# 906 more elements rest in free PSUM columns, and two loads are cut finer, in a decode kernel whose DMA engines never stop

## The chip, the cores and the metric

The kernel runs on one core of one Trainium2 chip. The metric is the device time of one execution in microseconds; lower is better. Times scatter by a few tenths of a microsecond between runs. Words used: HBM is the large memory that the loads read; SBUF and PSUM are the core's own memories; PSUM, divided into banks, takes the results of matmuls. In the views PE is TensorE (PEld its weight loads), DVE VectorE, ACT ScalarE, POOL GpSimd, SPq the queue of SyncE, which issues the loads. A load has landed when its last packet is in.

## The reference

Two layers, each attention and then a gated MLP, for one token. Only the last 4,096 positions of the caches count. Both layers use the same weights and the same caches.

```python
def _A_ref(x, k_cache, v_cache, wq, wo):            # Hq = Hkv = 32, Dh = 192, W = 4096, D = 640
    q = (x @ wq).reshape(B, Sq, Hq, Dh).transpose(0, 2, 1, 3)
    k = k_cache[:, :, Sk - W:, :]; v = v_cache[:, :, Sk - W:, :]
    p = softmax(einsum("bhqd,bhkd->bhqk", q, k) * Dh ** -0.5)
    return einsum("bhqk,bhkd->bhqd", p, v).transpose(...).reshape(B, Sq, Hq * Dh) @ wo
def _B_ref(x, w_gate, w_up, w_down):                # F = 1536
    return (sigmoid(x @ w_gate) * (x @ w_up)) @ w_down
x = A_x
for _ in range(2):
    x = x + _A_ref(layernorm(x), ...)
    x = x + _B_ref(layernorm(x), ...)
```

## The kernel before

Heads are treated in 16 pairs. A pair needs its query weights and keys ("a") and its values and output weights ("b"); each is about 7 MB for all 128 partitions. The bytes go by one DMA queue, issued by SyncE, into seven slots of SBUF and one region for the MLP's weights, cut into cells of 640 columns (`FW`). Some pairs stay in SBUF for layer 1. Of pair 1's values a part stays as well: it is copied into PSUM columns that nothing else uses ("stow"), and copied back in layer 1.

```python
stash = [(bank[i][:, c:c + n].bitcast(U32), 2 * n) for i, c, n in ((3, 0, NST // 2), (6, 0, NST // 2), (7, DC, 512 - DC))]
NSV = sum(n for _, n in stash)                      # 480 + 480 + 507 words: 2,934 bf16 elements a partition
...
MW = {..., "u2": (6, 7, 10), "u3": (9, 10, 12), "d2": (11, 6, 9), "d3": (14, 9, 12)}   # first cell, from block, to block
MV = {"v1": (17, len(rc)), "v0": (NSV // FW, 6), "v2": (6, 11), "v3": (11, 14), "v4": (14, 17)}   # cells of pair 1's values
VAFTER = {"v1": "u1", "v0": "d1", "v2": "u3", "v3": "d2", "v4": "d3"}     # issued when this piece of the MLP is consumed
...
def stow(i, after=()):                              # VectorE copies a part of pair 1's values out
    sv, o = B_SLOT[0][PM], sum(n for _, n in stash[:i])
    ev = pg.op("dve", lambda v: words(v, stash[i][0], slot(sv, v_at(PM) + o, stash[i][1])), rd=[rval[sv]], wr=[res(f"stash{i}")], own="st", after=after)
    rslot[sv].rd.append(ev)                         # the next load into this slot waits for the copy
def step(p, prev):
    if l == 0 and prev > 0:
        ev = PVn(prev - 1, 1 - prev % 2)            # output projection; frees the slot
    Q(p, 0); QK(p, 0); soft(0)
    if (l, prev) == (0, PM):                        # PM = 1
        stow(2, [ev])
    expo(); PVmm(prev, prev % 2); ET(p % 2); PVt(prev % 2)
    ...
def loop(p0, n):
    ...
            step(p + 1, p)
            if (l, p) == (0, PM):
                stow(0)
                stow(1)
```

A load into a slot is issued when all that used the slot is done. It then stands in the queue behind the bytes that were issued before it.

## Time and profile before

The kernel took 514.38 us (median of 3 runs). First the page of the kernel before: span, engine shares, the DMA row of the 40 slices (tenths busy), the packets, the bytes from HBM and the chain of waits by engine.

```profile
span 512.7 us, 8581 instructions
PE 263.9 (51%) x3716; PEld 138.7 (27%) x3716; DVE 100.3 (20%) x379; ACT 85.0 (17%) x171; POOL 4.2 (1%) x31
DMA  9999999999999999999999999999999999999996
DMA packets 9964, 218.71 MB, mean 427 GB/s; under 512 B 1240, under 2 KB 1368, under 8 KB 4952
HBM read 218.43 MB, written 0.00 MB: 426 GB/s over the span
DMA 63%; PE 24%; DVE 7%; ACT 3%; SPq 2%; issue 2%; DVEq 0%; POOL 0%; ACTq 0%; POOLq 0%
```

No compute engine is busy much over half of the time, and the DMA row is nines to the last slice. The DMA engines are the bound. The trace has a record of each packet with its start, its duration and its size. From these records, by packet size (bytes of one row), the median duration; the last column is what 16 engines move at that rate:

```
bytes of a packet   median us   x16 GB/s
            1,812       0.075        387
            2,560       0.102        402
            3,840       0.149        412
            6,400       0.244        420
           56,832       2.098        433
```

This is 8.4 ns plus 0.0368 ns a byte, to within 2 ns. A load of 128 rows puts 8 such packets and a semaphore write of 9 ns on each of the 16 engines. Between 5 and 506 us the engines have 16 packets in flight at every moment, to within 0.05 us.

Next the chain of waits of the kernel before, near the copies out and at the end (start, duration, what), and from the queue's own waits the one on a copy (total, times, longest).

```profile
55.67 0.22 DVE sh L511
55.90 1.14 DVE bank L170 x2
57.05 22.51 DMA big<-in_uc_dram
...
485.35 24.70 DMA big<-in_wd_dram
510.10 0.46 PE o L748 x6
```

```profile
SPq L214 <- DVE bank L170: 0.5, 1, 0.5
```

The two copies of line 170 end at 57.03 us, and only then is the next load issued. It lands 22.5 us later, behind the bytes that were issued before. The last load lands at 510.05 us; what follows is short and fixed.

### The profile page before, as it was taken

The page shows a single profiled execution, that of the slowest core. Times are in us where ns is not written, and L with a number is a line of the kernel's source. Part 1 is how long each engine was busy: PE and PEld are TensorE (multiplying, and loading weights), DVE is VectorE, ACT ScalarE, POOL GpSimd, SP SyncE. Part 2 cuts the span into 40 slices and gives each one's busy share as a digit, 9 for nine tenths or more (in the row PEclk, how much of TensorE's full clock was granted, in tenths as well). Part 3 has the DMA queues.
Part 4 walks back from the last instruction along what each step waited for, and adds up shares of the span by engine and source line. Part 5 has one row for each costly group of instructions (what it writes and reads, how often), then busy time and mean ns, then how long its engine had stood idle before and what let it go on. Part 6 is the DMA issues. An engine that isn't in the chain of part 4 may idle for free.

```text
span 512.7 us, 8581 instructions
## 1 busy us (share of the span) xinstructions
PE 263.9 (51%) x3716; PEld 138.7 (27%) x3716; DVE 100.3 (20%) x379; ACT 85.0 (17%) x171; POOL 4.2 (1%) x31
## 2 busy tenths in 40 slices
PE   0362455344643254445565777774625344634665
PEld 0221222122312122222234434532312122312334
DVE  0221212112210121112121243321202111210311
ACT  1110111011110111011120024130301011101220
POOL 0010000000000000000000000000000000000000
PEclk9955665566565775556575568765755566556565
DMA  9999999999999999999999999999999999999996
GB/s 431 426 423 426 427 430 428 430 461 439 426 430 426 435 430 426 443 457 430 394 420 415 419 438 441 434 425 425 461 439 435 426 426 430 445 426 417 427 429 273
DMA packets 9964, 218.71 MB, mean 427 GB/s; under 512 B 1240, under 2 KB 1368, under 8 KB 4952
## 3 DMA queue, kind: packets, MB, share of 16 engines
q1 hardware_dynamic: 9800, 218.37, 99.1%
q8 instruction: 13, 0.21, 0.1%
q10 hardware_dynamic: 144, 0.06, 0.0%
q14 instruction: 7, 0.06, 0.0%
HBM read 218.43 MB, written 0.00 MB: 426 GB/s over the span
## 4 chain that ended last, share of the span: by engine, by line
DMA 63%; PE 24%; DVE 7%; ACT 3%; SPq 2%; issue 2%; DVEq 0%; POOL 0%; ACTq 0%; POOLq 0%
DMA big<-in_uc_dram 54%; PE scores L430 8%; PE o L487 7%; DMA big<-in_wd_dram 6%; DMA big<-in_wu_dram 3%; DVE sc L440 3%; PE bank L446 2%; SPq L214 2%; PE bank L412 2%; ACT e_sb L454 2%; PE bank L522 1%; PE bank L460 1%; ACT diag L443 1%; DVE sc L472 1%; DVE qs L418 1%
## 5 line engine op out<-in xcount | busy, mean ns | idle before, releaser
L430 PE MATMUL scores<-big,qs 128*32 128x512 bf16 x744 | 82.9, 613 | 10.3 <-DVE qs L418 9.6
L412 PE MATMUL bank<-sh,big 128*128 128x1 bf16 x465 | 17.1, 166 | 132.5 <-DMA big<-in_uc_dram 130.1
L487 PE MATMUL o<-big,et_sb 128*2 128x384 bf16 x1024 | 78.1, 471 | 5.4 <-DMA big<-in_uc_dram 4.2
L443 ACT ACTIVATE diag<-cst,sc 128x128 f32<-128x128 bf16 x32 | 12.8, 401 | 307.9 <-DVE sc L440 292.3
L440 DVE TENSOR_REDUCE sc<-scores 128x1 f32<-128x1024 f32 x31 | 37.9, 1224 | 78.9 <-PE scores L430 78.9
L412 PEld LDWEIGHTS bank<-sh,big 128*128 128x128 bf16 x465 | 14.7, 104 | 135.6 <-DMA big<-in_uc_dram 113.4
L446 PE MATMUL bank<-diag,sc 128*128 128x128 f32 x64 | 22.7, 452 | 47.2 <-ACT diag L443 47.2
L454 ACT ACTIVATE e_sb<-scores,sc 128x1024 bf16<-128x1024 f32 x31 | 37.3, 1204 | 42.1 <-DVE sc L449 39.7
L487 PEld LDWEIGHTS o<-big,et_sb 128*2 128x2 bf16 x1024 | 28.6, 108 | 42.1 <-issue 29.8
L418 DVE TENSOR_TENSOR qs<-bank,cst 128x96 bf16<-128x96 f32 x30 | 7.7, 258 | 162.5 <-PE bank L412 162.5
L430 PEld LDWEIGHTS scores<-big,qs 128*32 128x32 bf16 x744 | 24.4, 133 | 43.8 <-issue 31.4
L446 PEld LDWEIGHTS bank<-diag,sc 128*128 128x128 f32 x64 | 14.2, 277 | 72.3 <-ACT diag L443 71.1
L494 ACT CAST o_sb<-o 128x384 bf16<-128x384 f32 x64 | 29.8, 473 | 21.2 <-PE o L487 21.0
L522 PE MATMUL bank<-sh,big 128*128 128x1 bf16 x480 | 17.1, 165 | 15.1 <-DVE sh L511 14.7
L464 DVE CAST et_sb<-bank 128x64 bf16<-128x64 f32 x32 | 7.2, 225 | 70.2 <-PE bank L460 70.2
L522 PEld LDWEIGHTS bank<-sh,big 128*128 128x128 bf16 x480 | 14.5, 99 | 17.6 <-DVE sh L511 12.3
L447 DVE TENSOR_REDUCE sc<-bank 128x2 f32<-128x128 f32 x32 | 9.3, 292 | 41.9 <-PE bank L446 41.9
L460 PEld LDWEIGHTS bank<-cst,e_sb 128*128 128x128 bf16 x256 | 8.9, 101 | 22.8 <-issue 16.3
L460 PE MATMUL bank<-cst,e_sb 128*128 128x8 bf16 x256 | 11.7, 169 | 6.6 <-ACT e_sb L454 6.5
L470 PE MATMUL o<-sc 128*128 128x2 f32 x62 | 13.8, 292 | 0.6 <-ACT o_sb L494 0.6
L470 PEld LDWEIGHTS o<-sc 128*128 128x128 f32 x62 | 11.9, 240 | 1.9 <-ACT o_sb L494 1.3
L472 DVE RECIPROCAL sc<-o 64x1 f32<-64x1 f32 x62 | 10.2, 164 | 9.4 <-PE o L470 7.7
(78 smaller groups left out, 107.8 us busy)
## 6 DMA issues: line engine op xcount, KB each, us to landing
big<-in_uc_dram SPq DMA_DIRECT2D x20, 7104.0 KB, 22.6
big<-in_uc_dram SPq DMA_DIRECT2D x11, 3552.0 KB, 21.4
big<-in_uc_dram SPq DMA_DIRECT2D x2, 3072.0 KB, 18.0
big<-in_uc_dram SPq DMA_DIRECT2D x7, 480.0 KB, 6.6
big<-in_uc_dram SPq DMA_DIRECT2D x4, 768.0 KB, 11.6
big<-in_uc_dram SPq DMA_DIRECT2D x1, 2048.0 KB, 11.1
big<-in_uc_dram SPq DMA_DIRECT2D x1, 2016.0 KB, 10.4
big<-in_wg_dram SPq DMA_DIRECT2D x4, 480.0 KB, 14.6
```

The source lines that it names most:

```text
L412: ins = t.matmul(qe[:, i:i + 1], lhsT=w[:, c * 2 * DH + c0:c * 2 * DH + c0 + P], rhs=xq[:, c:c + 1], start=(c == 0), stop=(c == DC - 1))
L430: ins = t.matmul(sc_x[1 + b][32 * j:32 * j + 32, :], lhsT=qs[:, y, k, :], rhs=slot(sa, WQE + k * W + (4 * b + j) * 512, 512), start=(k == ...
L440: pg.op("dve", lambda v: v.reduce_max(out=mx, in_=sc_x[0][:], axis=AX.X), wr=[res("mx")], ex=sc_x[3:5])
L443: pg.op("act", lambda a: a.mul(out=diag[:], in_=ident, mul=mx), rd=[res("cst"), res("mx")], wr=[res("diag")])
L446: pg.op("pe", lambda t: t.matmul(dmx[:, 0:P], lhsT=ones_f, rhs=diag[:], start=True, stop=True), rd=[res("diag"), res("ones")], ex=[rb[2]])
L454: pg.op("act", lambda a: a.activation(out=e_sb[:], in_=sc_x[0][:], func=ACT.Exp, bias=nbias, scale=srs_c, accum_out=rowsum), rd=[res("nbia ...
L460: ins = t.matmul(qe[:, 0:2 * NB].rearrange("p (r x) -> p r x", r=2)[:, :, 4 * b:4 * b + 4], lhsT=e_sb[:, b * P:(b + 1) * P], rhs=sel, star ...
L470: pg.op("pe", lambda t: t.matmul(sm, lhsT=ones_f, rhs=rs2[z], start=True, stop=True), rd=[res(f"rs2{z}"), res("ones")], wr=[res("rsum")], ...
L472: rb[bk].last["dve"] = pg.op("dve", lambda v, h=h: v.reciprocal(out=Rn[z][64 * h:64 * h + 64], in_=sm[64 * h:64 * h + 64, h:h + 1]), rd=[r ...
L487: ins = t.matmul(o8[h][32 * j:32 * j + 2, 0:2 * DH].rearrange("p (a d) -> p a d", a=2), lhsT=et_sb[:, z, h * NB + 2 * u:h * NB + 2 * u + 2 ...
L494: pg.op("act", lambda a, h=h: a.copy(out=o8_sb[:, :, h * DH:(h + 1) * DH], in_=o8[h][:, 0:2 * DH].rearrange("p (a d) -> p a d", a=2)), wr= ...
L522: ins = t.matmul(yT[:, j:j + 1], lhsT=wo[:, c * D + j * P:c * D + (j + 1) * P], rhs=oTb[z][:, c:c + 1], start=False, stop=(c == 2), skip_g ...
```

## The change

Its intent is fewer bytes. Three further ranges of PSUM columns (453 words) in banks 2, 4 and 5, which attention uses, take 906 elements of pair 1's values, so that the load "v0" of those elements falls away. The values that follow, and the last piece of the down weights, are loaded in smaller pieces, so that the queue is fed at shorter intervals. The new ranges must be copied back earlier in layer 1, before their banks are used.

```diff
-    stash = [(bank[i][:, c:c + n].bitcast(U32), 2 * n) for i, c, n in ((3, 0, NST // 2), (6, 0, NST // 2), (7, DC, 512 - DC))]
+    SB = [(3, 0, NST // 2), (6, 0, NST // 2), (7, DC, 512 - DC), (2, 264, 248), (4, 2 * DH + 2, 126), (5, 2 * DH, 79)]
+    stash = [(bank[i][:, c:c + n].bitcast(U32), 2 * n) for i, c, n in SB]
@@ loads
-          ... "d3": (14, 9, 12)}
+          ... "d3": (14, 9, 11), "d4": (16, 11, 12)}
-    MV = {"v1": (17, len(rc)), "v0": (NSV // FW, 6), "v2": (6, 11), "v3": (11, 14), "v4": (14, 17)}
-    VAFTER = {"v1": "u1", "v0": "d1", "v2": "u3", "v3": "d2", "v4": "d3"}
+    MV = {"v1": (17, len(rc)), "v0": (6, 9), "v2": (9, 11), "v3": (11, 14), "v4": (14, 17)}
+    VAFTER = {"v1": "u1", "v0": "u2", "v2": "u3", "v3": "d2", "v4": "d4"}
@@ copies out, layer 0 (soft calls `late` between its last two VectorE steps)
-            soft(0)
+            soft(0, late=(lambda: stow(3)) if (l, prev) == (0, PM) else None)
             if (l, prev) == (0, PM):
                 stow(2, [ev])
@@
                     if (l, p) == (0, PM):
-                        stow(0)
-                        stow(1)
+                        for i in (0, 1, 4, 5):
+                            stow(i)
@@ copies back, layer 1: right behind the first two query projections
+            for i in (3, 4, 5):
+                unstow(i)
@@
-        down("d2", "d3")
+        down("d2", "d3", "d4")
```

(The row sums move to another column of bank 2; the copy back becomes a function; "d4" gets the same condition for its issue as "d3".)

More of the change, by code (lines that the diff above doesn't have):

```diff
@@ L165, in decode_kernel @@
     o8, yT = bank[4:6], bank[7]
-    stash = [(bank[i][:, c:c + n].bitcast(U32), 2 * n) for i, c, n in ((3, 0, NST // 2), (6, 0, NST // 2), (7, DC, 512 - DC))]
+    SB = [(3, 0, NST // 2), (6, 0, NST // 2), (7, DC, 512 - DC), (2, 264, 248), (4, 2 * DH + 2, 126), (5, 2 * DH, 79)]
+    stash = [(bank[i][:, c:c + n].bitcast(U32), 2 * n) for i, c, n in SB]
     NSV = sum(n for _, n in stash)
+    assert NSV == 6 * FW
     def words(v, out, in_):
@@ L183, in decode_kernel @@
     MW = {"wg0": (0, 0, 3), "wg1": (3, 3, 6), "wg2": (6, 6, 9), "wg3": (9, 9, 12), "u0": (12, 0, 2), "u1": (14, 2, 7),
-          "d0": (0, 0, 3), "d1": (3, 3, 6), "u2": (6, 7, 10), "u3": (9, 10, 12), "d2": (11, 6, 9), "d3": (14, 9, 12)}
-    MAFTER = {"d0": ("wg0",), "d1": ("wg1",), "u2": ("wg2",), "u3": ("wg3",), "d2": ("wg3", "u0"), "d3": ("u1",)}
-    MV = {"v1": (17, len(rc)), "v0": (NSV // FW, 6), "v2": (6, 11), "v3": (11, 14), "v4": (14, 17)}
-    VAFTER = {"v1": "u1", "v0": "d1", "v2": "u3", "v3": "d2", "v4": "d3"}
+          "d0": (0, 0, 3), "d1": (3, 3, 6), "u2": (6, 7, 10), "u3": (9, 10, 12), "d2": (11, 6, 9), "d3": (14, 9, 11), "d4": (16, 11, 12)}
+    MAFTER = {"d0": ("wg0",), "d1": ("wg1",), "u2": ("wg2",), "u3": ("wg3",), "d2": ("wg3", "u0"), "d3": ("u1",), "d4": ("u1",)}
+    MV = {"v1": (17, len(rc)), "v0": (6, 9), "v2": (9, 11), "v3": (11, 14), "v4": (14, 17)}
+    VAFTER = {"v1": "u1", "v0": "u2", "v2": "u3", "v3": "d2", "v4": "d4"}
     PLACE = {s: i for i, s in enumerate((0, 3, 2, 1, 4, 5, 6))}
@@ L436, in QK, with soft @@
             return ev
-        def soft(x=0, hook=None, mid=None):
+        def soft(x=0, hook=None, mid=None, late=None):
             sc_x = S[x]
@@ L448, in soft @@
                   wr=[res("nb2")], ex=[rb[2]])
+            if late is not None:
+                late()
             pg.op("dve", lambda v: v.tensor_tensor_reduce(out=nbj, in0=nb2, in1=pm_s, scale=1.0, scalar=0.0, op0=ALU.mult, op1=ALU.add, accum_out=nbias),
@@ L468, in RS @@
         def RS(z, bk=4):
-            sm = bank[bk][:, 2 * DH:2 * DH + 2]
+            so = 260 if bk == 2 else 2 * DH
+            sm = bank[bk][:, so:so + 2]
             pg.op("pe", lambda t: t.matmul(sm, lhsT=ones_f, rhs=rs2[z], start=True, stop=True), rd=[res(f"rs2{z}"), res("ones")], wr=[res("rsum")], ex=[rb[bk]])
@@ L603, in attention, with unstow @@
             mark("QM", Q(PM, 1, 5))
+            def unstow(i):
+                o, n = sum(m for _, m in stash[:i]), stash[i][1]
+                pg.op("dve", lambda v: words(v, mreg(o, n), stash[i][0]), rd=[res(f"stash{i}")], wr=rc[o // FW:-(-(o + n) // FW)],
+                      ex=[rb[SB[i][0]]], own="st")
+            for i in (3, 4, 5):
+                unstow(i)
             ln_sq(xi)
@@ L615, in attention @@
             for i in (2, 0, 1):
-                o, n = sum(m for _, m in stash[:i]), stash[i][1]
-                pg.op("dve", lambda v, i=i, o=o, n=n: words(v, mreg(o, n), stash[i][0]), rd=[res(f"stash{i}")], wr=rc[o // FW:-(-(o + n) // FW)],
-                      ex=[rb[7]] if i == 2 else [], own="st")
+                unstow(i)
             expo(1)
```

## The prediction

> **What bounds the kernel now.** The 16 DMA engines. The page gives 218.71 MB at a mean of 427 GB/s and a DMA row of nines up to the last slice; PE is 51% busy, DVE 20%. By the trace's DMA packet records 16 packets are in flight at every moment from about 5 to 506 us (idle under 0.05 us per engine). The largest packets (56,832 bytes) take 2.098 us, 433 GB/s over 16 engines: the Trainium skill ("DMA: Bandwidth & Descriptors", "Where 436 GB/s comes from") puts the fabric's ceiling at 435 GB/s, and this trace agrees. So only engine time taken from the DMA queue shortens the kernel; the chain of waits, 63% DMA, says the same.
>
> **DMA cost, from the packet records.** A 128-row load is 8 packets and one semaphore write (9 ns) per engine. Packets of 1,812, 2,560, 3,840 and 6,400 bytes take 75, 102, 149 and 244 ns: about 8.4 ns plus 0.0368 ns a byte.
>
> - Removed: the load of 906 elements (1,812 bytes a row). With v2 (6,400) it becomes v0 (3,840) and v2 (2,560): before 8 x (75 + 244) = 2,552 ns, after 8 x (149 + 102) = 2,008 ns: -0.54 us per engine.
> - Added: d3 (3,840) becomes d3 (2,560) and d4 (1,280): about +0.08 us, an estimate from that fit.
> - Net: -0.46 us, all of it on the bound.
>
> **DVE, off the bound.** Six more copies, three out and three back. Today's take 650 ns for 480 words and 683 for 507 (groups by shape); I estimate 0.41, 0.28 and 0.23 us for 248, 126 and 79 words.
> - Out, near 55 us: in the timeline the load issued at 57.05 us waits for the last copy. It will go 0.5 to 0.9 us later. The queue then still holds about 2.8 us of work (my sum of issued minus served), and issue to first packet takes about 1.0 us (the first load). About 1 us of margin stays: no starvation.
> - Back, near 289.5 us: DVE is idle from 289.8 to 292.5 behind the first QK, so 0.9 us of copies fits.
>
> **The middle.** From 274.9 to 296 us (layer 0's MLP to layer 1's first pairs) each load is issued when a piece has been consumed, with 2.7 to 5.4 us of work queued. The 906 elements less shorten that by 0.6 us; the first value cells issued after u2 and the split of d3 give part back. I expect at least 2 us queued: no gap. The last down piece has 5 matmuls after its landing instead of 15, some 0.2 to 0.35 us off a PE chain that isn't the bound; not credited.
>
> **Prediction.** 514.38 - 0.46 = 513.9 us; the scatter of three runs (0.5 us) is as wide as the gain: 513.4 to 514.4. Faster by over 2%: 0.3%; within 2%: 99.4%; slower by over 2%: 0.3%.
>
> **What the profile would show.** HBM read 218.20 instead of 218.43 MB; the same DMA row of nines; a down load of 160 KB, none of 226.5 KB; the last load landing about 0.46 us earlier than 510.05 with the same 2.6 us after it; no landing before 284 us moved by over 0.1 us. Wrong steps would show as fewer than 16 packets in flight near 58 or 275 to 300 us, or PE waits on DVE copies near 290 us that delay the release of a slot while the queue is short.
>
> **What would make it wrong.** A starved queue after the late issue near 58 us or in the middle would eat the 0.46 us; run scatter of 0.3 us can hide or double it.

## The result and the profile after

The changed kernel took 514.01 us (median of 6 runs, 513.77 to 514.81), against 514.29 us (514.02 to 516.2) of the kernel before in the same rounds. The ratio is 0.9992, with a 95% interval from 0.9976 to 1.0008. Such ratios are worked out from the runs of the same rounds; they are not quite the ratios of the quoted medians. By the medians 0.28 us came off, by the ratio 0.4.

The page of the changed kernel, the same rows:

```profile
span 512.7 us, 8587 instructions
PE 260.1 (51%) x3716; PEld 136.8 (27%) x3716; DVE 102.1 (20%) x385; ACT 84.7 (17%) x171; POOL 4.2 (1%) x31
DMA  9999999999999999999999999999999999999996
DMA packets 10108, 218.47 MB, mean 426 GB/s; under 512 B 1256, under 2 KB 1384, under 8 KB 5096
HBM read 218.20 MB, written 0.00 MB: 426 GB/s over the span
DMA 63%; PE 23%; DVE 7%; ACT 3%; SPq 2%; issue 2%; DVEq 0%; POOL 0%; ACTq 0%; POOLq 0%
```

The 0.23 MB are gone, as planned, but this profile's span is no shorter. The chain of waits of the changed kernel at the same two places, and the queue's wait on a copy, show where to look:

```profile
56.15 0.22 DVE sh L516
56.37 1.12 DVE bank L172 x2
57.50 0.34 DVE o L172 x2
57.86 22.07 DMA big<-in_uc_dram
...
483.80 25.60 DMA big<-in_wd_dram
509.44 0.70 PE o L757 x16
510.18 0.47 PE o L757 x8
```

```profile
SPq L216 <- DVE o L172: 0.8, 1, 0.8
```

The load behind the copies is issued at 57.86 us instead of 57.05. The packet records of that load tell what came of it. Here are some of the packets of 56,832 bytes in the two traces (start, duration, end in us; the first packets of that load are those that start after 60.5 us):

```
kernel before                      changed kernel
58.644 2.098 -> 60.742             58.653 2.098 -> 60.751
58.892 2.098 -> 60.990             58.927 2.098 -> 61.025
60.505 2.098 -> 62.603             60.521 2.448 -> 62.969
60.656 2.098 -> 62.754             60.662 2.920 -> 63.582
60.777 2.098 -> 62.875             60.839 2.775 -> 63.614
60.992 2.098 -> 63.090             61.027 2.807 -> 63.834
61.951 2.098 -> 64.049             61.994 2.400 -> 64.394
```

In the changed kernel all of the first 16 packets of this load are slow: 0.17 to 0.82 us over the normal 2.098 us. The busy row doesn't show this, because such a packet counts as busy for all of its 2.3 to 2.9 us. I call the time over the median of the same size the loss. Summed over the load it is 0.56 us per engine, and 0.08 us of gaps come on top; the kernel before lost 0.005 us there. Two more loads of this trace, issued at 290.99 and 306.18 us, lost 0.14 and 0.17 us. Taken at normal durations, the packets of the whole kernel add up to 507.38 us per engine, against 507.85 before: 0.47 us less, and the prediction had 0.46. So the saving was made, and in this profile it was lost again. The balance closes. The last packets of the 16 engines (put in 16 rows from the starts and ends on record) end 0.36 us later on average than before, and that is 0.47 us saved against 0.67 us more of slow packets and 0.16 us more of gaps. About 0.6 us of this arose at the late load: the eleven loads that follow it, up to 253 us, all end about 0.55 us later than before (mean of the last 16 packets of each). About 0.3 us more arose between 250 and 320 us.

What the change cost on VectorE fits: the copies took 409, 283 and 233 ns where 0.41, 0.28 and 0.23 us had been estimated. On the way back PE waits for none of them. The timeline of the changed kernel in layer 1 (start, duration, engine, line, operation):

```profile
289.90 2.75 PE L432 MATMUL scores<-big,qs 128*32 128x512 bf16 x24
290.07 0.41 DVE L172 TENSOR_SCALAR big<-bank 128x248 uint32<-128x248 uint32 x1
290.51 0.57 DVE L172 TENSOR_SCALAR big<-o 128x126 uint32<-128x126 uint32 x2
...
292.59 0.56 PE L414 MATMUL bank<-sh,big 128*128 128x1 bf16 x15
```

The copies lie behind the first scores, as predicted, and PE's next group follows them without a pause.

### The profile page after: what moved, and what is told of

Its sections match the earlier page's. It is cut to its first block, busy times and chain, and to the rows that moved or that the text cites. A ratio compares the mean times of both kernels' runs of the same rounds, so it can differ in the third digit from the quotient of the medians. Undisturbed runs are those within 1.5% of the kernel's fastest.

```text
span 512.7 us, 8587 instructions
## 1 busy us (share of the span) xinstructions
PE 260.1 (51%) x3716; PEld 136.8 (27%) x3716; DVE 102.1 (20%) x385; ACT 84.7 (17%) x171; POOL 4.2 (1%) x31
## 3 DMA queue, kind: packets, MB, share of 16 engines
HBM read 218.20 MB, written 0.00 MB: 426 GB/s over the span
## 4 chain that ended last, share of the span: by engine, by line
DMA 63%; PE 23%; DVE 7%; ACT 3%; SPq 2%; issue 2%; DVEq 0%; POOL 0%; ACTq 0%; POOLq 0%
DMA big<-in_uc_dram 54%; PE scores L432 8%; DMA big<-in_wd_dram 6%; PE o L492 6%; DVE sc L442 3%; DMA big<-in_wu_dram 3%; PE bank L448 2%; ACT e_sb L458 2%; SPq L216 2%; PE bank L414 2%; PE bank L527 1%; PE bank L464 1%; ACT diag L445 1%; DVE sc L477 1%; DVE qs L420 1%
## 5 line engine op out<-in xcount | busy, mean ns | idle before, releaser
L432 PE MATMUL scores<-big,qs 128*32 128x512 bf16 x744 | 81.8, 607 | 10.3 <-DVE qs L420 9.6
L492 PE MATMUL o<-big,et_sb 128*2 128x384 bf16 x1024 | 74.9, 456 | 6.0 <-DMA big<-in_uc_dram 3.4
L492 PEld LDWEIGHTS o<-big,et_sb 128*2 128x2 bf16 x1024 | 27.1, 104 | 41.0 <-issue 26.0
```

Of the source, the lines that this page charges most:

```text
L432: ins = t.matmul(sc_x[1 + b][32 * j:32 * j + 32, :], lhsT=qs[:, y, k, :], rhs=slot(sa, WQE + k * W + (4 * b + j) * 512, 512), start=(k == ...
L492: ins = t.matmul(o8[h][32 * j:32 * j + 2, 0:2 * DH].rearrange("p (a d) -> p a d", a=2), lhsT=et_sb[:, z, h * NB + 2 * u:h * NB + 2 * u + 2 ...
```

## The experiments

Three theories stood after the first profile. Theory 1: the load behind the copies is issued too late, and its first packets wait. Theory 2, a rival: the queue, shorter by 906 elements between 275 and 310 us, starves there. Theory 3: nothing is lost, the rest is scatter of the runs. Kernels are compared only within the same rounds.

### The changed kernel again

> The changed kernel unaltered, a second profile and five more rounds. Theory 1 (the load that waits for the last copy out is issued 0.8 us later, at 57.9 us, and its first packets wait): the same loss again, 0.4 to 0.6 us of packet time per engine in the load issued near 57.9 us, and a time 0.1 to 0.4 us under the kernel before. Theory 2 (short queue in the middle, 285 to 310 us): losses there of about 0.3 us again. Theory 3 (nothing is lost, run scatter only): no such loss in this profile, and 0.46 us under the kernel before.

Measured: 513.84 us (513.55 to 514.19) against 514.27; ratio 0.9988 (0.9974 to 1.0001). This profile shows no loss near 60 us (0.003 us), and none over 0.05 us between 250 and 320 us. Its last load lands at 509.71 us, 0.34 before that of the kernel before. So theories 1 and 2 both missed with their expectation of the same loss again, and what theory 3 expected came out (no loss, and 0.43 us under the kernel before): the loss doesn't come in every execution. Why the same program issued that load at 57.12 us this time and at 57.86 the first time is seen in the copies' surroundings. The timelines of PE and SyncE, first profile and then second:

```profile
52.30 2.73 PE L492 MATMUL o<-big,et_sb 128*2 128x384 bf16 x32
57.86 0.33 SPq L216 DMA_DIRECT2D big<-in_uc_dram  x1
```

```profile
51.77 1.70 PE L492 MATMUL o<-big,et_sb 128*2 128x384 bf16 x32
57.12 0.33 SPq L216 DMA_DIRECT2D big<-in_uc_dram  x1
```

The matmuls ahead of the copies took 2.73 us in the one and 1.70 us in the other. The stretch from 51.5 to 55 us in each (busy time of the engines, then PEclk, DMA share and GB/s), again first and then second profile:

```profile
51.50:55.00 3.50, 3.43 (x35) 1.47 (x36) 1.29 (x5) 1.68 (x4) 0.00 (x0) 0.50 1.20 520
```

```profile
51.50:55.00 3.50, 2.95 (x50) 1.79 (x50) 1.71 (x8) 2.04 (x4) 0.00 (x0) 0.70 1.20 520
```

The mean granted clock of the stretch was 0.50 and 0.70. The Trainium skill ("TensorE: Matmul & The Clock Gate", "Part 1: The HAM clock gate") says that PE starts throttled and that activity releases it; it names a half-rate and a full-rate state. The traces agree on the two states: the clock records of all 13 profiles hold 0.50 and 1.00 alone, means lie between them (a stretch can hold both), and in a third profile, below, the clock was 1.00 here and the group took 1.47 us. That activity releases the clock was not tested here. So when a DMA load goes out depends, through the wait for the slot, on the clock that PE happened to be granted. By the chains of waits this makes about 0.53 of the 0.74 us between the two issues; the other 0.21 us is there from the start, because the load that this pair waits for landed at 46.09 us in the first profile and at 45.88 us in the second.

### Copies out earlier, in the changed kernel

All six copies go where VectorE has nothing to do: behind the queries of pair 2, while PE computes its scores.

```diff
-            soft(0, late=(lambda: stow(3)) if (l, prev) == (0, PM) else None)
             if (l, prev) == (0, PM):
-                stow(2, [ev])
+                for i in (0, 1, 2, 3, 4, 5):
+                    stow(i, [ev] if i == 2 else ())
+            soft(0)
@@ loop
-                    if (l, p) == (0, PM):
-                        for i in (0, 1, 4, 5):
-                            stow(i)
```

> The changed kernel with all six copies out moved into the time in which VectorE waits for the scores of pair 2 (46.7 to 49.6 us), so that no copy is the last thing the load waits for. Theory 1: that load goes at about 56.5 us, the loss near 60 us falls from 0.56 to under 0.1 us per engine, and the time falls to 0.4 to 0.6 us under the kernel before. Theory 2: the load goes earlier but the losses at 285 to 310 us stay, and the time stays 0.1 to 0.4 us under the kernel before. Theory 3: no difference from the changed kernel.

Measured: 513.66 us (513.59 to 513.8) against 514.27; ratio 0.9984 (0.9970 to 0.9998). The timeline of VectorE, PE and SyncE (in square brackets the engine's idle time before and what ended it):

```profile
46.49 2.12 DVE L172 TENSOR_SCALAR bank<-big 128x480 uint32<-128x480 uint32 x4
46.63 2.75 PE L432 MATMUL scores<-big,qs 128*32 128x512 bf16 x24 [0.35 <-DVE qs L420]
48.51 0.42 DVE L172 TENSOR_SCALAR o<-big 128x126 uint32<-128x126 uint32 x2
49.43 1.22 DVE L442 TENSOR_REDUCE sc<-scores 128x1 f32<-128x1024 f32 x1 [0.49 <-PE scores L432]
...
51.56 1.47 PE L492 MATMUL o<-big,et_sb 128*2 128x384 bf16 x32
55.69 0.33 SPq L216 DMA_DIRECT2D big<-in_uc_dram  x1
```

The copies fit under the scores, the reduction starts when the scores are done, and the load is issued at 55.69 us (at the full clock), over a microsecond earlier than in the kernel before. It lost nothing, nothing was lost between 250 and 320 us (apart from some 0.03 us around each fetch of instructions, which all profiles have), and the last load landed at 509.59 us. That is 0.46 us earlier than in the kernel before: the whole saving. The middle of this kernel is that of the changed one, so its shorter queue does not cost time in every execution. This is what theory 1 expected; but the second profile of the changed kernel lost nothing either, so one profile without a loss doesn't show that the early copies prevent it.

### Copies out earlier, in the kernel before

The same edit with the three copies of the kernel before.

> The kernel before with its three copies out moved to the same place. It lost under 0.05 us per engine in that load, so theory 1 expects the issue about 0.6 us earlier (near 56.4 us) and no change of the time, within 0.15 us. If it gets faster by 0.3 us or more, the early copies help by something else than the loss near 60 us.

Measured: 514.31 us (514.02 to 514.37) against 514.27; ratio 0.9996 (0.9982 to 1.0010). The load was issued at 56.76 us (clock low, the matmul group took 2.73 us) and the last load landed at 510.11 us. As expected, an earlier issue gains nothing where nothing was lost.

### Copies out later, in the kernel before: two doses

```diff
-                        stow(0)
-                        stow(1)
+                        for i in (0, 1, 0, 1):          # first dose; (0, 1, 0, 1, 0, 1) is the second
+                            stow(i)
```

> The kernel before with the two copies that the load waits for made twice (same bytes loaded, same result). Theory 1: the load is issued at about 58.2 us in place of 57.05, its first packets lose 0.8 to 1.0 us per engine, and the time grows by 0.4 to 1.0 us. Theories 2 and 3: the time is that of the kernel before within 0.15 us.

Measured: 514.53 us (514.07 to 515.46) against 514.27; ratio 1.0006 (0.9992 to 1.0020). The profiled run had the full clock ahead of the copies (matmul group 1.47 us), so that the issue moved only to 57.39 us; the loss there was 0.11 us, most of it in two packets, although the first packet came 3.21 us after the issue, and the last load landed at 510.06. The expected issue near 58.2 us did not occur in this profile, and the time is not resolved from that of the kernel before.

> The kernel before with the two copies that the load waits for made three times (2.3 us more of VectorE ahead of the load's issue; same bytes, same result). From the profiles so far the load loses nothing when issued by 57.1 us, 0.11 us per engine at 57.39 and 0.64 us (packets and gaps) at 57.86. Theory 1: issue between 58.4 and 59.4 us by the granted clock of that moment, a loss of 1.1 to 2.1 us per engine at 60 to 63 us, and a time 0.8 to 2.0 us over the kernel before. Rivals (short queue in the middle, or scatter only): no change over 0.2 us.

Measured: 515.22 us (514.39 to 516.35) against 514.14; ratio 1.0026 (1.0014 to 1.0038), so longer by 1.1 us by the medians, and the interval excludes 1. The load was issued at 59.68 us, a little later than the expected 58.4 to 59.4. The timeline:

```profile
52.09 2.73 PE L487 MATMUL o<-big,et_sb 128*2 128x384 bf16 x32
52.61 0.68 DVE L170 TENSOR_SCALAR bank<-big 128x507 uint32<-128x507 uint32 x1
56.20 3.45 DVE L170 TENSOR_SCALAR bank<-big 128x480 uint32<-128x480 uint32 x6
59.68 0.33 SPq L214 DMA_DIRECT2D big<-in_uc_dram  x1
```

So a late issue here costs time: the bytes loaded are the same, and the program is slower. The size of the loss surprised. The load came 1.8 us later than in the changed kernel's first profile, yet its packets lost 0.47 us and the gaps were 0.06 us, not 1.1 to 2.1 us. Its first packet started 0.99 us after the issue. So about 1 us is enough for a first packet to start, as the prediction had it, but not for it to run at its normal speed; and the changed kernel's first profile, whose load had its first packet 2.66 us after the issue, lost time although it was issued in time by that measure. (The last load of the second dose landed 0.90 us later than that of the kernel before. On the average of the 16 engines the last packets end 0.62 us later: 0.54 us more of slow packets, nearly all in this load, and 0.06 us of gaps. The other 0.28 us is the slowest engine, further behind the average than before, and is not explained.)

### Only the bytes

The load of the 906 elements is left out of the kernel before, with nothing in its place. The values are wrong (the comparison with the reference passed all the same, so its tolerance doesn't see them).

```diff
-    ... "v1", "wq2", "v0", "v2", "v3", "v4", ...
+    ... "v1", "wq2", "v2", "v3", "v4", ...
```

> The kernel before without the load of the 906 elements and without any copy in its place; the result is wrong on purpose. This is the removed cost by itself: 8 packets of 75 ns and one semaphore write, 0.61 us per engine. If bytes on the DMA engines are the bound: 0.5 to 0.7 us under the kernel before. If the queue, 0.6 us shorter in the middle, starves there: packets lose time between 285 and 310 us and the gain is under 0.4 us.

Measured: 513.56 us (513.4 to 514.42) against 514.14; ratio 0.9990 (0.9977 to 1.0003). At normal durations the packets add up to 507.24 us, 0.61 us less, as computed. By the median 0.58 us came off, though the interval includes 1. But the profiled run was the slowest of the five (514.42), and its trace shows theory 2's starvation: a load issued at 285.46 us with its first packet only 1.03 us later, 0.93 us of loss per engine between 286 and 296 us and 0.30 us of gaps. So the short queue in the middle is a real danger, here where nothing was done against it.

### Early copies, loads not cut finer

```diff
-          ... "d3": (14, 9, 11), "d4": (16, 11, 12)}
+          ... "d3": (14, 9, 12)}
-    MV = {... "v0": (6, 9), "v2": (9, 11), "v3": (11, 14), "v4": (14, 17)}
+    MV = {... "v2": (6, 11), "v3": (11, 14), "v4": (14, 17)}
-    VAFTER = {... "v0": "u2", "v2": "u3", "v3": "d2", "v4": "d4"}
+    VAFTER = {... "v2": "u3", "v3": "d2", "v4": "d3"}
```

> The changed kernel with the early copies, and with the loads not cut finer: the last down piece whole, the values behind it in one load after u3 (two loads fewer). By the packet sum 0.15 us less per engine than the early version. If the finer loads are needed to keep the queue filled: losses at 285 to 310 us of more than that, and a time 0 to 0.4 us over the early version. If not: 0.1 to 0.2 us under the early version.

Measured: 513.54 us (513.45 to 513.81) against 514.14; ratio 0.9990 (0.9977 to 1.0003). The packet sum is 507.24 us, 0.14 us below that of the early version, as computed. Its profile lost 0.29 us per engine between 286 and 296 us; the early version's lost nothing there beyond the fetch of instructions. The last load landed at 509.64 us against 509.59. In these two profiles the finer loads cost 0.14 us of packets and spared 0.29 us of loss; the last landings are 0.05 us apart, and the times don't resolve it.

### Early copies and 226 further elements

```diff
-    SB = [(3, 0, NST // 2), (6, 0, NST // 2), (7, DC, 512 - DC), (2, 264, 248), (4, 2 * DH + 2, 126), (5, 2 * DH, 79)]
+    SB = [(3, 0, 512), (6, 0, 512), (2, 264, 248), (4, 2 * DH + 2, 126), (5, 2 * DH, 128), (7, DC, 512 - DC)]
```

(and the indices of the copies accordingly)

> The changed kernel with the early copies and 226 further elements in the 113 columns still free (banks 3 and 6: 32 each, bank 5: 49), 4,066 elements at rest in all. The first value load shrinks from 3,840 to 3,388 bytes a row, 0.13 us less per engine by the packet fit. Expected 0.1 to 0.2 us under the early version, so 0.6 to 0.8 us under the kernel before; correct result; no loss near 58 us.

Measured: 513.58 us (513.53 to 513.77) against 514.14; ratio 0.9989 (0.9977 to 1.0002). The packet sum is 507.25 us, 0.13 us below the early version's. By the medians it is 0.56 us under the kernel before, just short of the expected 0.6 to 0.8. One load, issued at 257.84 us, lost 0.30 us.

### Three of them once more

> The changed kernel a third time, for its scatter on one chip beside the early version. Its load at 57 to 58 us is issued by chance late (57.86) or early (57.12), by the granted clock at 52 us. Expected: 513.8 to 514.1 us median, a range of five runs of 0.5 us or more; in the profile a loss over 0.1 us in that load only if it is issued later than about 57.4 us.

Measured: the changed kernel 513.82 us (513.53 to 514.07) against 514.26; ratio 0.9992 (0.9978 to 1.0005). Clock 1.00 ahead of the copies, issue at 56.82 us, loss there 0.07 us, last landing 509.62 us. All of this is within the expectation.

> The early version again. Expected: 0.2 to 0.4 us under the changed kernel of the same rounds, the five runs within 0.3 us, that load issued by 56.9 us whatever the clock, no loss in it.

Measured: the early version 513.73 us (513.41 to 515.09); ratio 0.9994 (0.9981 to 1.0008). Issue at 55.74 us, no loss there, last landing 509.55 us. One of its five runs took 515.09 us, against the expectation of a range of 0.3 us, and its median is only 0.09 us under that of the changed kernel. The reason for that run is not known; it was not the profiled one.

> The early version with 226 elements more, again. By its packet sum 0.13 us under the early version; the first time it was 0.03 us nearer the kernel before than the version with whole pieces, with 0.30 us lost in one load issued at 257.8 us. If that loss was chance: 0.05 to 0.2 us under the early version now.

Measured: the version with 226 more elements 513.57 us (513.53 to 513.77); ratio 0.9987 (0.9973 to 1.0001). That is 0.16 us under the early version, as expected, but its profile lost again in the same load, issued at 257.78 us, 0.17 us this time, and its last load landed at 509.63 us. So that loss was not chance alone: in both profiles of this version the first packet of that load came early, 2.69 and 2.71 us after the issue.

### All loads of all profiles together

For every load issued between 5 and 470 us in all 13 profiles, the time from its issue to its first packet (how long it stood in the queue) and the loss in its first 16 packets:

```
issue to first packet   loads   mean loss us   largest   loads that lost over 0.1 us
under 1.5 us                2          0.304      0.43      2
1.5 to 2.3 us               7          0.051      0.18      1
2.3 to 2.6 us              24          0.010      0.13      1
2.6 to 2.8 us              40          0.035      0.47      5
2.8 us and more           673          0.002      0.07      0
```

No load that had stood 2.8 us in the queue lost over 0.1 us in its first 16 packets. Below that, 9 of 73 did. The limits of the rows were chosen after the loads had been seen, and 2.8 us is not a sharp limit: over all their packets some loads that had stood longer lost too (0.11 us after 3.21 us in the first dose, 0.17 us after 3.11 us in the kernel with only the bytes). The table leaves out the first 5 us, and what stands there matters most. The very first load of the kernel meets an empty queue; in all 13 profiles its first packet started 1.01 to 1.04 us after the issue, and its first 16 packets lost 0.51 to 0.70 us. So each load here that met an empty queue did lose (these, the one of the second dose, and the one of the bytes-only kernel), though the start of a kernel may differ in other ways too; and the trace from which the prediction read its 1.0 us shows 0.59 us of loss in the same load. The skill ("DMA: Bandwidth & Descriptors", "Latency and other measured facts") gives about 0.6 us to the first byte and an HBM access of 0.2 us on average and 2 us at high load. That is of the right size: 0.6 and 2 us make an estimated 2.6 us (from that page), and the queue here is at full load; but five of the nine loads had stood 2.6 to 2.8 us, longer than that. No run here looks inside the wait, so this cause is argued and not shown; nor is it shown what decides which loads lose, or how much (0.43 us in the first 16 packets after 0.99 us in the queue, 0.47 us after 2.66 us).

The kernels in one view (medians; the kernel before is that of the same rounds):

| kernel | us | before | median under before | last landing in the profile |
|---|---|---|---|---|
| changed, three times | 514.01 / 513.84 / 513.82 | 514.29 / 514.27 / 514.26 | 0.28 / 0.43 / 0.44 | 510.14 / 509.71 / 509.62 |
| early copies, twice | 513.66 / 513.73 | 514.27 / 514.26 | 0.61 / 0.53 | 509.59 / 509.55 |
| early, pieces whole | 513.54 | 514.14 | 0.60 | 509.64 |
| early, 226 more, twice | 513.58 / 513.57 | 514.14 / 514.26 | 0.56 / 0.69 | 509.67 / 509.63 |
| before, early copies | 514.31 | 514.27 | -0.04 | 510.11 |
| before, bytes only (wrong values) | 513.56 | 514.14 | 0.58 | 510.51 |
| before, late copies, two doses | 514.53 / 515.22 | 514.27 / 514.14 | -0.26 / -1.08 | 510.06 / 510.95 |

The early versions beat the kernel before in every comparison of medians, by 0.53 to 0.69 us. Over the changed kernel they gain 0.1 to 0.2 us by the medians, which these intervals do not resolve. Among themselves they are not told apart. For the changed kernel itself the interval of each set includes 1, but the three sets together leave little doubt that it is faster: 14 of its 16 runs are under 514.24 us, the median of the 35 runs of the kernel before, and 9 are under the fastest of these (513.99 us).

## Why the prediction was right or wrong, point by point

- **The bound: right.** With fewer bytes the kernel got shorter, and the largest increase found (the second dose) came about mostly through the DMA queue.
- **The cost of the loads: right.** -0.46 us per engine was predicted; the packets at normal durations gave -0.47. HBM read 218.20 MB as stated, one down load of 160 KB came and that of 226.5 KB went.
- **The time: right in size.** 513.9 us was predicted. The three sets of the changed kernel gave 514.01, 513.84 and 513.82 us; all 16 runs have a median of 513.91. This tests little by itself: the predicted 513.4 to 514.4 also holds the kernel before (514.24), and in the first profile the saving had been made and lost again while the time was still in the range.
- **"About 1 us of margin stays: no starvation", near 58 us: this step failed in part.** The lead that would be left was right (about 2.8 us predicted, 2.66 measured). The delay was right (0.5 to 0.9 us predicted, 0.81 in the first profile, 0.07 in the second, and a gain of 0.23 in the third, by the clock). The need was under-sized: issue to first packet of about 1.0 us, read from the first load of the kernel, is the time in which a first packet starts (0.99 us again in the second dose), not the time after which it runs at its normal speed: that first load itself lost 0.59 us in its first 16 packets. Packets that were issued with 2.66 us in hand lost 0.56 us per engine. In place of 1.0 us the losses seen begin below some 2.8 us, so there was no margin. It cost 0.56 us and 0.08 us of gaps in one profile of three, more than the whole saving.
- **The middle: right in two profiles of three.** At least 2 us queued was expected; the shortest time from issue to first packet between 274 and 300 us was 2.34, 2.69 and 2.62 us in the three profiles (2.59 before). "No gap" held in two; the first lost 0.14 and 0.17 us in two loads, with gaps of 0.10 us; their first packets came 2.69 and 2.47 us after the issue. At least 2 us queued was too little to rule out a loss, for the same reason as near 58 us.
- **VectorE's copies: right,** to the nanosecond nearly, and PE waited for none on the way back. The residual after the MLP started 0.37 us after the last landing (287.39 to 287.76), against 0.64 before (286.46 to 287.10): 0.27 us, in the predicted 0.2 to 0.35.
- **"No landing before 284 us moved by over 0.1 us": wrong,** and careless. The third load of the kernel, which the change doesn't touch, landed at 45.83, 46.09, 45.88 and 45.79 us in the four profiles. Landings scatter by 0.3 us between runs of one program, so such a line can't be a test.

## What to carry to other kernels

When the DMA queue is the bound, ask of every load how long it will have stood in the queue before its first packet, and keep that over the value below which losses are seen (some 2.8 us here, though most loads below it lost nothing), not over the time in which the first packet of an empty queue starts; the loss doesn't show as an idle engine but as slow first packets. What delays the release of a buffer (here, copies that could run in an idle stretch of VectorE and a matmul group whose speed hangs on the granted clock) belongs ahead of the critical release (what that gains, 0.1 to 0.2 us here, was not resolved), and a gain of a tenth of a per cent should be read from packet sums and several profiles, as one profile may show it whole and the next not at all.

## What the Trainium skill lacked or had wrong

- "DMA: Bandwidth & Descriptors" gives a first-byte latency (about 0.6 us for HWDGE) and an HBM latency, but no lead that a load needs behind a full queue. Here, of loads that stood under 2.8 us in the queue 9 of 73 lost over 0.1 us per engine in their first 16 packets; of 673 that stood longer none did.
- The same page has no cost of a HWDGE packet by size. Here it is 8.4 ns plus 0.0368 ns a byte (75 ns for 1,812 bytes, 2,098 ns for 56,832), the same in the traces before and after. Its ceiling of 435 GB/s agrees with the 433 GB/s of the largest packets.
- "Perfetto Trace Analysis", "DMA Engine Tracks", says that the slices of a DMA engine show actual busy time without idle time. The packet records here seem to hold waiting as well: packets of 56,832 bytes, 2.098 us otherwise, are recorded with 2.3 to 2.9 us after a late issue, and the DMA row stays at nines in the profile that lost 0.56 us per engine in one load. That the excess is waiting is argued from the late issue; no run looks inside a packet.
